# Third and fourth quarter's z: half of the reload moved from GpSimd's to ScalarE's queue and behind K's last spectra, three buffers instead of two, and a lower planned rate for those spectra

## The chip, the cores and the metric

The kernel runs on one core of one Trainium2 chip. The metric is the device time of one execution in microseconds (us). The kernel before has a median of 581.79 us in three runs (581.66 to 582.94).

## What is computed

Two independent blocks whose results are laid side by side. Block A is an FNet mixing layer, block B a long convolution (an S4D state-space layer), both for a sequence of 2048 and a width of 512, in float32:

```python
# A: y = Real(DFT_seq(DFT_hidden(x)))
a = einsum("bsd,ed->bse", x, dft_hid_re);  b = einsum("bsd,ed->bse", x, dft_hid_im)
y_A = einsum("ts,bse->bte", dft_seq_re, a) - einsum("ts,bse->bte", dft_seq_im, b)
# B: a convolution kernel K from the state-space parameters, applied by FFT
P = exp((A * dt[:, None])[:, :, None] * pos);  K = 2.0 * einsum("dn,dnl->dl", C, P).real
Kf = rfft(K, 2 * L);  Uf = rfft(u.transpose(0, 2, 1), 2 * L)
y_B = irfft(Uf * Kf, 2 * L)[:, :, :L].transpose(0, 2, 1) + u * D_skip
out = concatenate([y_A, y_B], axis=-1)
```

## The kernel before

**Block A** (`Fnet`) is dense matrix multiplication. Every float32 operand is split into a high and a low part: ScalarE writes `hi<-raw` (line 226), VectorE `lo<-raw,hi` (line 230), and three matmuls of 128x512 (line 371) make one product: `hi,x_hi`, `lo,x_hi`, `hi,x_lo`. Eight groups with the sequence matrix write intermediate tiles `p` to DRAM, and four last groups read them back as `raw<-p` (line 339, SyncE's queue), eight tiles to a group, and store `out_ya` (line 405). Four split tiles (`hi`, `lo`) exist at a time, so each `hi<-raw` waits until TensorE has used up the tile four before.

**Block B** (`Ssm`) builds K's taps with tables on VectorE and ScalarE, transforms u and K by an FFT in two stages, and works through the 512 channels in four quarters of 128 (`h` = 0 to 3). The parts near the change are these:

- `store_k` (line 879) writes the first stage of K's transform to DRAM, `xk<-xk_sb`. `load_spectrum` (line 990) reads u's and K's spectra back, four pieces (`q` = 0 to 3) to a quarter. For the last quarter the pieces go into 16 tiles that block A no longer needs, `x_hi8`, `x_lo8` to `x_hi15`, `x_lo15`, so K's last spectra are 16 transfers `x_hi<-xk` and `x_lo<-xk` of 128 KB, in rows of 128 floats (512 bytes), four to a piece, all on SyncE's queue.
- `product` makes the second stage with TensorE (line 1035, `f<-xt,w` or `f<-x_hi,w`), copies it with ScalarE (line 1014, `uk<-f`), multiplies the spectra on VectorE (lines 1019 to 1055), starts the inverse transform on TensorE (line 1062, `f<-uk,ia`), copies that with ScalarE (line 1077, `z<-f`), and `store_z` writes it to DRAM (line 1086, `zs<-z`, rows of 512 bytes). All these steps take turns in two pairs of PSUM banks, `f0` and `f1`: a step on TensorE waits until ScalarE has emptied the pair of the step before.
- `inverse2` (third and fourth quarter, `h` = 2 and 3) reads z back and finishes. A quarter has two passes, `i` = 0 and 1, and each pass loads 1 MB into a tile `zl` of 128 partitions: partitions 0 to 63 by one transfer of 512 KB on SyncE's queue, partitions 64 to 127 by another of 512 KB on GpSimd's queue (both line 1118), in rows of 1024 floats (4 KB). VectorE then adds and subtracts (lines 1124, 1126: `zsum<-zl`, `zl<-zl`), TensorE multiplies (line 1133, `f<-zsum,ib` and `f<-zl,ib`), ScalarE copies (line 1138, `zl<-f`), and the result is stored as `out_yb<-zl` (line 1141). The tiles `zl` and `zsum` have two buffers, so the fourth quarter's passes wait for the third quarter's stores.

**What sets the order.** A planner (`Plan`) runs all these steps as coroutines before the program is built. A step yields an engine and an estimated duration; the planner always takes the step that can start first, and the instructions are written out in that order. Each engine then runs its own instructions strictly in this order and waits by semaphores. A transfer is planned on one resource `"dma"` with a size and a rate: `load(512, 270)` stands for 512 KB at 270 KB per us. Planned numbers set only the order; no instruction waits for a planned time. A plan `Event` in the same way only holds a step back in the plan and leaves no semaphore behind.

All transfers on SyncE's and on ScalarE's queue share eight completion semaphores in turn, over both queues. A transfer therefore also waits until the one eight before it in the written order has landed. GpSimd's transfers have semaphores of their own.

Of the kernel before, what the change touches and what calls it, by code (L numbers as in the profile page):

```python
# [8 lines left out]
F32 = mybir.dt.float32  # L9
# [8 lines left out]
PART = DM // 4  # L18
# [57 lines left out]
class Sem:  # L76


    def __init__(self, n):
        self.free, self.waiting = [0.0] * n, []  # L80
# [107 lines left out]
def act(cols):  # L188
    return 0.09 + cols * 0.00085


def dve(cols, rate=1.0):
    return (66 + cols / rate) / 960


def load(kb, rate=330):
    return max(0.55, kb / rate)
# [211 lines left out]
class Buffers:  # L409


    def __init__(self, pool, n):
        self.pool, self.n = pool, n
        self.xts, self.uks, self.zbs, self.zls = Sem(1), Sem(n), Sem(n), Sem(n)


class Joined(Event):
# [18 lines left out]
class Ssm:  # L436
# [506 lines left out]
    def quarters(self):  # L943


        self.plan.spawn(self.constants(1, self.const2_ev), 3)
        self.zs_left, self.xt = [4] * 4, {}
        self.xt_ev = {(n, h, q): Event() for n in "uk" for h in range(4) for q in range(4)}
        self.take_ev = {(h, q): Event() for h in range(4) for q in range(4)}
        self.plan.spawn(self.take(), 1)  # L950
        xu = [self.xu[:, :, :, PART * h:PART * h + PART] for h in range(4)]
        self.plan.spawn(self.spectra("u", xu, [[self.xu_ev] * 2] * 4), 1)
        self.plan.spawn(self.spectra("k", [self.xk[h] for h in range(4)], self.xk_ev), 1)
        self.plan.spawn(self.products(), 1)
        self.ib2_ev = Event()
        self.plan.spawn(self.load_ib2(), 1)
        for h in range(4):
            self.plan.spawn(self.inverses(h), 1)
# [24 lines left out]
                self.plan.spawn(self.load_spectrum(name, h, q, view), 1)  # L983

    def load_spectrum(self, name, h, q, view):
        yield "dma", load(512, 270), FAST
        for r in range(2):
            for p, xt in enumerate(self.xt[h, q][r]):
                n = xt.shape[1]
                self.nc.sync.dma_start(xt[:, :, "uk".index(name)], view[2 * q + r, :, n * p:n * p + n])  # L990
        self.plan.set(self.xt_ev[name, h, q])

    def products(self):
        for h in range(4):
            yield self.set_ev[h // 3]
            b = self.sets[h // 3]
            for q in range(4):
                for n in "uk":
                    yield self.xt_ev[n, h, q]
                yield b.uks  # L1000
                got = yield from self.banks(2)
                done = Event()
                self.plan.spawn(self.product(b, h, q, got, done), LATE[h] if h < 3 else LAST)
                yield done
# [105 lines left out]
    def inverse2(self, b, h, i, n):  # L1110

        nc, c = self.nc, n // 2
        z = b.pool.tile([128, 2, c, PART], F32, name="zl", bufs=b.n)
        view = self.zs[h].rearrange("(a s) c l d -> (s c) a l d", a=2)
        yield "pool", ISSUE
        for y, e in enumerate((nc.sync, nc.gpsimd)):
            o = n * i + c * y
            e.dma_start(z[64 * y:64 * y + 64], view[:, :, o:o + c])
        yield "dma", load(64 * n, 270), FAST if h == 3 else None
        t = b.pool.tile([128, c, PART], F32, name="zsum", bufs=b.n)  # L1120
        for w in range(0, c, 4):
            m = slice(w, w + 4)
            yield "dve", dve(512)
            nc.vector.tensor_tensor(t[:, m], z[:, 0, m], z[:, 1, m], op=OP.add)
            yield "dve", dve(512), *APART
            nc.vector.tensor_tensor(z[:, 1, m], z[:, 0, m], z[:, 1, m], op=OP.subtract)
        (k, ps), = yield from self.banks(1)
        yield "pe", 1.06, None, 64
        for o in range(0, c, 2):
            for x in range(4):  # L1130
                for y in range(2):
                    r, w = slice(64 * y, 64 * y + 64), o + x // 2
                    nc.tensor.matmul(ps[32 * x:32 * x + 32, y, PART * (o // 2):PART * (o // 2) + PART],
                                     self.ib2[r, c * i + w, x % 2], (t, z[:, 1])[x % 2][r, w], start=True, stop=True,
                                     tile_position=(64 * y, 32 * x))
        for y in range(2):
            yield "act", act(512)
            nc.scalar.activation(z[:, 0, 4 * y:4 * y + 4].rearrange("p w d -> p (w d)"), ps[:, y], AF.Copy)
        self.give(k)
        yield "dma", load(32 * n, 270)  # L1140
        nc.sync.dma_start(self.out[:, c * i:c * i + c, PART * h:PART * h + PART], z[:, 0])
        self.plan.put(b.zls)
# [28 lines left out]
ISSUE = 1.0  # L1171
# [76 lines left out]
```

## Time and profile before

| what | value |
|---|---|
| median of three runs | 581.79 us |
| the profiled execution's own time | 582.32 us |
| its span in the profile | 580.5 us |
| TensorE (PE) busy | 570.5 us, 98% of the span |
| VectorE (DVE) busy | 523.0 us, 90% |
| ScalarE (ACT) busy | 371.2 us, 64% |
| GpSimd (POOL) busy | 42.5 us, 7% |
| moved by DMA | 133.70 MB, mean 230 GB/s |
| mean granted TensorE clock | 0.997 |

The profile is of one execution. Its span runs from the first to the last recorded instruction; the execution's own time, 582.32 us, is 1.8 us longer, and 0.53 us above the median of the three runs. Times in the rows are microseconds from the span's start. PE is TensorE's matmul side, PEld its weight loads, SPq and ACTq are the DMA issues on SyncE's and ScalarE's queue; DMA issues don't count as busy time. A row of the timeline gives the start, the duration, the engine, the line, the operation, the output and inputs, how many were merged, and in brackets how long the engine had been idle and what ended that.

### The profile page before, as it was taken

The numbers are of one execution on the slowest core, as the hardware profiler recorded it, in microseconds if no ns is written. First come the engines' busy times: TensorE is split into PE (matmuls) and PEld (weight loads), VectorE is DVE, ScalarE is ACT, GpSimd is POOL, SyncE is SP. The second block draws the span as 40 slices with busy tenths as digits, with TensorE's granted clock in tenths as the row PEclk, the third lists the DMA queues.
The fourth block names the chain that finished last, engine by engine and source line by source line (L and its number), as shares of the span: only waits on it lengthen the run. The fifth ranks groups of instructions, "written<-read, shape, count | busy, mean of one in ns | idle before, by whom it ended". The sixth has DMA issues, their size and how long they took to land.

```text
span 580.5 us, 15679 instructions
## 1 busy us (share of the span) xinstructions
PE 570.5 (98%) x6278; PEld 433.6 (75%) x6278; DVE 523.0 (90%) x928; ACT 371.2 (64%) x728; POOL 42.5 (7%) x64
## 2 busy tenths in 40 slices
PE   8999999999999999999999999999999999989997
PEld 6877767788777777778777777777787777756685
DVE  7999999999999999999999999999989999346742
ACT  5779665763777595768568585945688745335632
POOL 0001000000100000000000001001100000000000
PEclk9999999999999999999999999999999999989999
DMA  8899999996569767866796887479999995799784
GB/s 276 309 370 259 288 281 275 282 274 169 134 159 240 201 178 219 205 170 213 205 224 190 235 218 225 126 184 295 249 286 268 234 295 165 183 237 302 211 231 146
DMA packets 147976, 133.70 MB, mean 230 GB/s; under 512 B 47296, under 2 KB 107328, under 8 KB 147648
## 3 DMA queue, kind: packets, MB, share of 16 engines
q1 hardware_dynamic: 138976, 115.54, 66.8%
q0 software_dynamic: 8640, 16.78, 14.4%
q8 instruction: 49, 0.80, 0.6%
q10 hardware_dynamic: 288, 0.39, 0.2%
q14 instruction: 23, 0.19, 0.1%
HBM read 89.95 MB, written 42.73 MB: 229 GB/s over the span
## 4 chain that ended last, share of the span: by engine, by line
PE 59%; DVE 26%; DMA 6%; issue 5%; ACT 2%; SPq 1%; DVEq 0%; ACTq 0%
PE acc L371 46%; DVE prod L613 8%; DVE t L622 5%; PE f L1035 4%; DVE lo L230 4%; PE f L809 3%; PE f L1062 3%; DMA xk<-xk_sb 2%; DMA x_lo<-xk 2%; DVE t L642 1%; DMA raw<-in_sT 1%; DMA xu<-zl 1%; PE f L858 1%; PE f L1155 1%; DVE z L1019 1%
## 5 line engine op out<-in xcount | busy, mean ns | idle before, releaser
L371 PE MATMUL acc<-hi,x_hi 128*128 128x512 f32 x640 | 258.9, 404 | 0.1
L371 PE MATMUL acc<-lo,x_hi 128*128 128x512 f32 x640 | 250.7, 392 | 0.0
L371 PE MATMUL acc<-hi,x_lo 128*128 128x512 f32 x640 | 250.1, 391 | 0.0
L613 DVE TENSOR_TENSOR prod<-t,cs 128x1024 f32<-128x1024 f32 (+4 forms) x192 | 163.3, 869 | 1.7 <-ACT t L731 0.6
L371 PEld LDWEIGHTS acc<-hi,x_hi 128*128 128x128 f32 x640 | 120.6, 188 | 50.2 <-issue 24.2
L371 PEld LDWEIGHTS acc<-hi,x_lo 128*128 128x128 f32 x640 | 120.5, 188 | 26.2 <-DVE x_lo L230 0.3
L371 PEld LDWEIGHTS acc<-lo,x_hi 128*128 128x128 f32 x640 | 120.8, 189 | 23.1 <-DVE lo L230 0.2
L226 ACT ACTIVATE hi<-raw 128x512 fp32r<-128x512 f32 x132 | 82.6, 628 | 65.4 <-PE acc L371 48.0
L230 DVE TENSOR_TENSOR lo<-raw,hi 128x512 fp32r<-128x512 f32 x132 | 90.2, 685 | 23.9 <-ACT hi L226 23.7
L622 DVE TENSOR_TENSOR t<-prod 128x512 f32<-128x512 f32 (+4 forms) x192 | 94.3, 513 | 1.0
L629 ACT ACTIVATE square<-t 128x256 f32<-128x256 f32 (+1 forms) x64 | 36.7, 573 | 32.1 <-DVE t L622 29.3
L1014 ACT ACTIVATE uk<-f 128x1024 f32<-128x1024 f32 x32 | 31.2, 1018 | 17.7 <-PE f L1035 17.7
L325 POOL DMA_DIRECT2D lo<-in_sT x28 | 24.5, 874 | 213.3 <-ACT lo L323 44.2
L396 ACT ACTIVATE y<-acc 128x512 f32<-128x512 f32 x47 | 28.0, 595 | 11.0 <-PE acc L371 10.8
L809 PEld LDWEIGHTS f<-t,t 128*32 128x32 f32 x2048 | 29.5, 110 | 6.9 <-issue 4.7
L809 PE MATMUL f<-t,t 128*32 128x64 f32 x2048 | 32.4, 220 | 0.9 <-DVE t L622 0.4
L1019 DVE TENSOR_TENSOR z<-uk 128x512 f32<-128x512 f32 x32 | 21.9, 686 | 10.3 <-ACT uk L1014 9.5
L320 POOL DMA_DIRECT2D hi<-in_sT x28 | 15.8, 566 | 189.5 <-PE acc L371 113.2
L1077 ACT ACTIVATE z<-f 128x512 f32<-128x512 f32 x32 | 17.7, 590 | 12.6 <-PE f L1062 10.4
L642 DVE TENSOR_TENSOR t<-square 128x128 f32<-128x128 f32 (+1 forms) x64 | 24.8, 387 | 0.0
L1035 PE MATMUL f<-xt,w 64*32 64x256 f32 x768 | 23.5, 379 | 0.0
L1021 DVE TENSOR_TENSOR uk<-uk 128x512 f32<-128x512 f32 x32 | 22.1, 690 | 1.0
(102 smaller groups left out, 506.5 us busy)
## 6 DMA issues: line engine op xcount, KB each, us to landing
raw<-in_sT SPq DMA_DIRECT2D x99, 256.0 KB, 5.2
p<-y SPq DMA_DIRECT2D x32, 256.0 KB, 3.3
xk<-xk_sb SPq DMA_DIRECT2D x32, 256.0 KB, 5.3
zs<-z SPq DMA_DIRECT2D x32, 256.0 KB, 4.0
raw<-p SPq DMA_DIRECT2D x32, 256.0 KB, 4.2
hi<-in_sT POOLq DMA_DIRECT2D x28, 256.0 KB, 4.6
lo<-in_sT POOLq DMA_DIRECT2D x28, 256.0 KB, 5.0
xt<-xu SPq DMA_DIRECT2D x24, 256.0 KB, 4.9
```

The costliest lines, as they stand in the source:

```text
L226: self.nc.scalar.activation(hi, src, AF.Copy)
L230: self.nc.vector.tensor_tensor(lo, src, hi.bitcast(F32), op=OP.subtract)
L371: nc.tensor.matmul(acc[d], l[:, cols], r, start=k == 0 and n == 0, stop=k == len(items) - 1 and n == 2)
L396: self.nc.scalar.activation(y, ps, AF.Copy, scale=-1.0 if g[2] == 1 else 1.0)
L613: self.nc.vector.tensor_tensor(p.rearrange("p k d c m -> p k (d c) m"), src.rearrange("p d c l -> p (d c) l")[:, None, :, rows].to_broadca ...
L622: self.nc.vector.tensor_tensor(dst[:, :, :, rows], p[:, 0], p[:, 1, :, ::-1], op=OP.add)
L629: self.nc.scalar.activation(sq, t[:, :, :, m // 2:m], AF.Square)
L642: self.nc.vector.tensor_tensor(t[:, :, 0, m:2 * m:2], box[0][:, :, 0], box[0][:, :, 1], op=OP.subtract)
L809: nc.tensor.matmul(ps[32 * j:32 * j + 32, i], t1[:, d, c], t2[:, d, c], start=c == 0, stop=c == 1, tile_position=(0, 32 * j))
L1014: a.activation(uk[:, r].rearrange("p g c n d -> p g (c n d)"), p, AF.Copy)
L1019: v.tensor_tensor(P[0][:, r], t[:, r], u[:, r], op=OP.mult)
L1035: nc.tensor.matmul(got[r][1][32 * xx:32 * xx + 32, g, 256 * c:256 * c + 256], self.w2[rows, 2 * q + r, xx, 32 * c:32 * c + 32], xt[rows].r ...
```

## The change

Four edits, all in block B.

1. **The queue of z's second half.** In `inverse2` the transfer of partitions 64 to 127 is issued by ScalarE instead of GpSimd, planned as a step of 0.5 us on ScalarE ahead of the transfer's own planned time. The first half stays on SyncE's queue, but is written out after the planned transfer time is granted and not with the second half.
2. **The place of the third quarter's.** For `h` = 2 the plan holds these steps back until K's last spectra (`"k"`, quarter 3, piece 3) are planned, by the new event `loaded_ev`.
3. **Buffers.** `zl` and `zsum` of the last stage have three buffers instead of two (`2 * b.n - 1` with `b.n` = 2), and the plan's semaphore for them three places. In the earlier stage `b.n` is 1 and nothing changes.
4. **The planned rate.** K's spectra of the last quarter are planned at 200 KB per us instead of 270.

```diff
-        self.xts, self.uks, self.zbs, self.zls = Sem(1), Sem(n), Sem(n), Sem(n)
+        self.xts, self.uks, self.zbs, self.zls = Sem(1), Sem(n), Sem(n), Sem(2 * n - 1)
...
     def load_spectrum(self, name, h, q, view):
-        yield "dma", load(512, 270), FAST
+        yield "dma", load(512, 200 if h == 3 and name == "k" else 270), FAST
...
         self.plan.set(self.xt_ev[name, h, q])
+        if (name, h, q) == ("k", 3, 3):
+            self.plan.set(self.loaded_ev)
...
-        z = b.pool.tile([128, 2, c, PART], F32, name="zl", bufs=b.n)
+        z = b.pool.tile([128, 2, c, PART], F32, name="zl", bufs=2 * b.n - 1)
         view = self.zs[h].rearrange("(a s) c l d -> (s c) a l d", a=2)
-        yield "pool", ISSUE
-        for y, e in enumerate((nc.sync, nc.gpsimd)):
-            o = n * i + c * y
-            e.dma_start(z[64 * y:64 * y + 64], view[:, :, o:o + c])
+        if h == 2:
+            yield self.loaded_ev
+        yield "act", 0.5
+        nc.scalar.dma_start(z[64:], view[:, :, n * i + c:n * i + n])
         yield "dma", load(64 * n, 270), FAST if h == 3 else None
-        t = b.pool.tile([128, c, PART], F32, name="zsum", bufs=b.n)
+        nc.sync.dma_start(z[:64], view[:, :, n * i:n * i + c])
+        t = b.pool.tile([128, c, PART], F32, name="zsum", bufs=2 * b.n - 1)
```

The written order differs from before only from the first piece of the fourth quarter on. Three places show it. Numbers behind names tell tiles apart; they are not the same numbers in the two kernels. Lines from 992 on are two to three higher in the changed kernel.

**TensorE, where the fourth quarter begins** (`f<-x_hi8`, `f<-x_lo8` are the first piece of K's and u's last spectra, `acc` is block A). Before:

```order
L371 MATMUL acc_6782<-hi_6684,x_hi0_5234 128x512
L371 MATMUL acc_6782<-lo_6685,x_hi0_5234 128x512
L371 MATMUL acc_6782<-hi_6684,x_lo0_5235 128x512
L1035 MATMUL f1_6734<-x_hi8_6013,w2_113 32x256 x4
L1035 MATMUL f1_6734<-x_lo8_6014,w2_113 32x256 x4
```

After:

```order
L371 MATMUL acc_6778<-hi_6684,x_hi0_5234 128x512
L371 MATMUL acc_6778<-lo_6685,x_hi0_5234 128x512
L371 MATMUL acc_6778<-hi_6684,x_lo0_5235 128x512
L371 MATMUL acc_6761<-hi_6708,x_hi1_5443 128x512
L371 MATMUL acc_6761<-lo_6709,x_hi1_5443 128x512
L371 MATMUL acc_6761<-hi_6708,x_lo1_5444 128x512
L1037 MATMUL f1_6734<-x_hi8_6013,w2_113 32x256 x4
L1037 MATMUL f1_6734<-x_lo8_6014,w2_113 32x256 x4
```

Three more matmuls of block A (one product) stand ahead of the first piece, and the pieces behind it follow three later too. Further on, 15 matmuls of block A stand between the third and the fourth piece's `f<-uk,ia` where there were 12, and 12 between the third quarter's two passes where there were three.

**ScalarE, from the third piece's `uk<-f` to the last piece's `z<-f`.** Before:

```order
L226 ACTIVATE hi_7011<-raw_6701 128x512
L1077 ACTIVATE z_7030<-f1_6991 128x2x2x128
L1077 ACTIVATE z_7030<-f0_6999 128x2x2x128
L1014 ACTIVATE uk_7046<-f1_7039 128x1024
L1014 ACTIVATE uk_7046<-f0_7045 128x1024
L226 ACTIVATE hi_7093<-raw_6720 128x512
L1077 ACTIVATE z_7123<-f1_7088 128x2x2x128
L1077 ACTIVATE z_7123<-f0_7096 128x2x2x128
L226 ACTIVATE hi_7134<-raw_6769 128x512
```

After:

```order
L226 ACTIVATE hi_7005<-raw_6701 128x512
L1120 DMA zl_6950<-zs_107 64x2x1024
L1120 DMA zl_6951<-zs_107 64x2x1024
L1079 ACTIVATE z_7029<-f1_6994 128x2x2x128
L1079 ACTIVATE z_7029<-f0_6999 128x2x2x128
L226 ACTIVATE hi_7053<-raw_6720 128x512
L1016 ACTIVATE uk_7049<-f1_7042 128x1024
L1016 ACTIVATE uk_7049<-f0_7048 128x1024
L226 ACTIVATE hi_7135<-raw_6769 128x512
L1079 ACTIVATE z_7127<-f1_7092 128x2x2x128
L1079 ACTIVATE z_7127<-f0_7099 128x2x2x128
```

The third quarter's two transfers stand between a split and the second piece's `z<-f`, and two splits stand ahead of a copy that they stood behind. The fourth quarter's two (`zl_7230`, `zl_7262`) stand on ScalarE directly behind the third quarter's last copy `zl<-f`, with one split between them and three behind. GpSimd's four transfers of line 1118 are gone, and GpSimd has nothing left to do there.

**SyncE's queue, from the first piece's `zs<-z` to the third piece's.** Before:

```order
L1086 DMA zs_107<-z_6929 128x4x128
L339 DMA raw_6972<-p3_1_1_94 128x512
L1118 DMA zl_6910<-zs_107 64x2x1024
L1118 DMA zl_6911<-zs_107 64x2x1024
L339 DMA raw_7034<-p3_1_2_95 128x512
L1086 DMA zs_107<-z_7030 128x4x128
L1086 DMA zs_107<-z_7123 128x4x128
```

After:

```order
L1088 DMA zs_107<-z_6929 128x4x128
L339 DMA raw_6973<-p3_1_1_94 128x512
L1122 DMA zl_6950<-zs_107 64x2x1024
L1088 DMA zs_107<-z_7029 128x4x128
L339 DMA raw_7034<-p3_1_2_95 128x512
L339 DMA raw_7090<-p3_1_3_96 128x512
L1122 DMA zl_6951<-zs_107 64x2x1024
L1088 DMA zs_107<-z_7127 128x4x128
```

(Each `zs<-z` is two transfers that read alike; one is shown.) The second pass's first half (`zl_6951`) now stands behind the second piece's store and two block-A loads, and that store stands behind one z transfer instead of two.

More of the change, by code (lines that the diff above doesn't have):

```diff
@@ L954, in quarters @@
         self.plan.spawn(self.products(), 1)
-        self.ib2_ev = Event()
+        self.ib2_ev, self.loaded_ev = Event(), Event()
         self.plan.spawn(self.load_ib2(), 1)
```

## Prediction

> **What bounds the kernel now.** The page first: its first part names the busiest engine.
>
> ```profile
> PE 570.5 (98%) x6278; PEld 433.6 (75%) x6278; DVE 523.0 (90%) x928; ACT 371.2 (64%) x728; POOL 42.5 (7%) x64
> ```
>
> TensorE (PE) is busy for 570.5 of 580.5 us, so an edit that leaves the matmuls alone can win only where PE waits or runs slowly. The waits of PE, longest first, show where:
>
> ```profile
> PE f L1035 <- DMA x_hi<-xk: 1.7, 1, 1.7
> ...
> PE f L1035 <- DMA x_lo<-xk: 1.0, 1, 1.0
> ```
>
> Both are in one place, the first piece of the fourth quarter, where the second stage of K's transform waits for K's last spectra. The timeline of PE around it:
>
> ```profile
> 511.49 0.39 PE L371 MATMUL acc<-hi,x_lo 128*128 128x512 f32 x1
> 511.80 0.42 PE L1035 MATMUL f<-x_hi,w 64*32 64x256 f32 x4
> ...
> 514.59 0.64 PE L1035 MATMUL f<-x_hi,w 64*32 64x256 f32 x8 [1.69 <-DMA x_hi<-xk]
> 516.25 0.63 PE L1035 MATMUL f<-x_lo,w 64*32 64x256 f32 x4 [1.03 <-DMA x_lo<-xk]
> ...
> 521.13 0.42 PE L1035 MATMUL f<-x_hi,w 64*32 64x256 f32 x4
> ...
> 525.28 1.12 PE L1062 MATMUL f<-uk,ia 32*64 32x256 f32 x32
> ```
>
> The stretch from a piece's first `f<-x_hi` through the nine `acc` matmuls behind it appears twice. Undisturbed it lasts 525.28 - 521.13 = 4.15 us, with the waits 521.13 - 511.80 = 9.33 us. The disturbance costs 5.18 us, more than its 1.69 + 1.03 = 2.72 us of idle time. The table by stretches shows part of the rest (after PE's and PEld's busy time: DVE, ACT, POOL, then granted clock, DMA share, GB/s):
>
> ```profile
> 510.00:515.00 5.00, 3.31 (x49) 1.89 (x47) 2.29 (x4) 1.96 (x3) 0.00 (x0) 1.00 1.04 194
> 515.00:520.00 5.00, 3.97 (x35) 2.22 (x30) 1.17 (x3) 1.02 (x1) 0.00 (x0) 0.66 1.14 235
> ...
> 535.00:540.00 5.00, 5.00 (x79) 3.37 (x77) 2.00 (x4) 2.57 (x4) 0.00 (x0) 1.00 1.05 231
> 540.00:545.00 5.00, 5.00 (x74) 3.36 (x76) 4.96 (x9) 2.25 (x4) 0.00 (x0) 1.00 0.29 82
> ```
>
> Right behind the waits the granted clock averages 0.66 over 5 us, which is 0.34 x 5 = 1.70 us of work lost. The last 0.76 us are matmuls of the piece that normally overlap in pairs and were pulled apart.
>
> Why are the spectra late? The issues on SyncE's queue and GpSimd's, in order of time:
>
> ```profile
> 505.98 0.37 SPq L990 DMA_DIRECT2D x_hi<-xk  x1
> ...
> 506.91 0.46 SPq L990 DMA_DIRECT2D x_hi<-xk  x1
> 507.42 0.47 SPq L990 DMA_DIRECT2D x_lo<-xk  x1
> ```
> ```profile
> 507.43 1.26 POOL L1118 DMA_DIRECT2D zl<-zs  x2 [64.27 <-ACT y L396]
> ```
>
> These three take 3.8, 7.5 and 8.8 us from issue to landing, by the DMA view of a window around each issue:
>
> ```profile
> x_hi<-xk SPq DMA_DIRECT2D x1, 128.0 KB, 3.8
> ```
> ```profile
> x_hi<-xk SPq DMA_DIRECT2D x1, 128.0 KB, 7.5
> ```
> ```profile
> x_lo<-xk SPq DMA_DIRECT2D x1, 128.0 KB, 8.8
> ```
>
> What lies between them is GpSimd's issue of the third quarter's z halves, 1 MB in rows of 4 KB. By queue (packets, MB, share of the 16 engines' time), from 509 to 516 us:
>
> ```profile
> q0 software_dynamic: 265, 0.99, 73.1%
> q1 hardware_dynamic: 871, 0.42, 28.9%
> ```
>
> In these 7 us GpSimd's queue (q0) moves z's megabyte, and SyncE's queue (q1), which holds the spectra, gets 28.9% and 0.42 MB. That z is used only in the third quarter's passes, far behind (the chain further down); it comes early, and in the way.
>
> **The change part by part.** I count on the clock of before, as if the disturbance were there, and subtract it at the end.
>
> *Z leaves 507 us.* ScalarE's timeline of before shows the two steps between which z's halves now stand:
>
> ```profile
> 532.88 0.63 ACT L226 ACTIVATE hi<-raw 128x512 fp32r<-128x512 f32 x1 [1.10 <-PE acc L371]
> 534.02 1.09 ACT L1077 ACTIVATE z<-f 128x512 f32<-128x512 f32 x2 [0.50 <-PE f L1062]
> ```
>
> So they are issued behind a split that ran at 532.88, 25 us after GpSimd's issue. Nothing else but block A's loads shares the engines with K's spectra, so I take 3.8 us for the first piece's others too: the last, issued at 507.42, lands at 511.2. PE asks for it at 511.80 + 0.66 for the three matmuls put ahead = 512.5 at the earliest. The wait of 2.72 us goes, with the pulled-apart pairs and the low clock: -5.18 us. The lower planned rate matters only through those three matmuls, which are moved, not added: 0. From below: at 7.5 us it would land at 514.9; 2.4 us of waiting would stay, and 1.70 for the clock: 4.1.
>
> [...]
>
> *Two issues on ScalarE.* No row has this shape on ScalarE; on SyncE the same transfer takes 0.60 us to issue, at most 1.21.
>
> ```profile
> L1118 SPq DMA_DIRECT2D zl<-zs x4: 579/601/1205, 529.8 to 556.5; - x4
> ```
>
> Queued behind them is the second piece's `z<-f`, possible from 534.02 + 0.66 = 534.68. The split ends between 533.5 and 534.2 (it may move by 0.66 too); 1.2 us of issues make that 534.7 to 535.4, and the copy ends by 536.5. The fourth piece, which needs the banks, starts at 536.83 (next rows). Cost 0; at 1.21 us each up to 0.9 us; a gain is excluded, since PE has no gap here (5.00 of 5.00 from 535 to 540).
>
> *Z in its new place.* The chain from 536 us, in order of time:
>
> ```profile
> 536.17 1.89 PE f L1035 x64
> 538.05 2.29 PE acc L371 x9
> 540.35 1.05 PE f L1062 x32
> 541.40 2.95 PE acc L371 x12
> 544.35 1.05 PE f L1062 x32
> 545.39 1.59 PE acc L371 x6
> 546.99 1.09 PE f L1133 x64
> ```
>
> Three more matmuls are 2.95 - 2.29 = 0.66 us. In the new order the fourth piece starts at 536.83, its `f<-uk` at 536.83 + 1.89 + 2.29 + 1.05 + 2.95 + 0.66 = 545.67, the third quarter's first pass at 545.67 + 1.05 + 1.59 = 548.31, the second at 548.31 + 1.09 + 2.95 = 552.35.
>
> The tight one is the third piece's `z<-f`: it reuses a tile whose store, `zs<-z` of the second piece, must have landed, and it empties the banks for `f<-uk` at 545.67. It lasts 1.09 us, so the store may land at 544.58.
>
> ```profile
> 542.00 1.09 ACT L1077 ACTIVATE z<-f 128x512 f32<-128x512 f32 x2 [2.25 <-DMA zs<-z]
> ```
> ```profile
> 535.13 8.89 SPq L1086 DMA_DIRECT2D zs<-z  x4
> ```
> ```profile
> q1 hardware_dynamic: 318, 1.00, 101.3%
> ```
>
> Before, it was issued at 535.13 and landed at 542.00, behind 1 MB of z and one load. The third row is the queue's from 533 to 538 us: full, at 1.00 MB in 5 us. Now 1.5 MB of z compete with it, and the load (0.26 MB) stands behind: 542.00 + 0.66 + 0.52 / 0.2 - 0.26 / 0.2 = 543.96 (0.52 MB is one transfer). That is 0.6 us early: cost 0, and a store that landed sooner would win nothing, since PE has no gap there. Its cover is thin. From above I take the slowest spectrum under GpSimd's traffic, the last number here:
>
> ```profile
> DMA to landing us min/median/max: 3.2/7.0/10.3
> ```
>
> The pair's second store, issued some 0.5 us behind the first as the spectra are, would then land at 535.13 + 0.66 + 0.5 + 10.3 = 546.6, and PE would wait 546.6 + 1.09 - 545.67 = 2.0 us, plus 1.70 for the clock: 3.7.
>
> The second pass's first half now waits on SyncE's queue for a split after 536.83 (0.63 us, and about as long on VectorE) and is issued near 539. Z transfers take at most 10.4, and a step of VectorE's on z takes 0.68:
>
> ```profile
> DMA to landing us min/median/max: 7.2/8.3/10.4
> ```
> ```profile
> 565.88 0.68 DVE L1124 TENSOR_TENSOR zsum<-zl 128x512 f32<-128x512 f32 x1
> ```
>
> So it lands by 549.4, VectorE's four steps end at 549.4 + 2.7 = 552.1, and PE asks at 552.35. Cost 0; each us later would cost one.
>
> *The tail and the third buffer.* From here PE has the same work in the same order as before.
>
> ```profile
> 568.00 1.09 PE f L1133 x64
> ...
> 571.38 1.09 PE f L1133 x64
> ```
>
> Before, the last pass's z was there at 565.88 at the latest, VectorE needs 2.7 us, and PE asked at 571.38: 2.8 us of slack. ScalarE now issues behind the third quarter's last copy (552.35 + 1.09 + 1.09 = 554.5), the last by about 556.5. The third buffer lets the first go without the third quarter's store, and GpSimd's queue is left empty. Queued behind it are splits that PE first needs 42 matmuls after 553.44, at 0.22 us each near 562.7. Cost 0.
>
> The sum: the profiled execution's 582.32 - 5.18 = 577.14; the median lies 0.53 below that execution, so **576.6 us**.
>
> **The rivals.**
>
> *The congestion moves* (0.20). Z's megabyte shares the engines with stores in rows of 512 bytes, as it did with spectra; the DMA share from 535 to 540 is 1.05 already. The store lands past 544.58 and PE waits at 545.67. For it: a margin of 0.6 us. Against it: from 540 to 545 the share is 0.29, 3.5 us of room. Time from 577.2, where a wait of 0.6 us would show, to 576.6 + 3.7 = 580.3. [...]
>
> *The low clock stays* (0.04). If it came from no wait, 1.70 us remain: 578.3. [...] Against it: 0.66 stands in the stretch of the waits and 1.00 in those around it.
>
> *The spectra stay late* (0.06): the change would not do what it says. They wait for something else, and only the three matmuls help: 581.79 - 0.66 = 581.1. Against it: 3.8 us to landing against 7.5 us, with issues 0.93 us apart and GpSimd's traffic between them.
>
> *Slower: the fourth quarter's reload* (0.06). Two queues now carry its 2.1 MB beside two results `out_yb` of 0.52 MB and two `out_ya` of half that, 3.7 MB in all, after a stretch that is fuller than before. If they went at 0.2 MB per us from 552.35, z would be there at 570.9; VectorE's 2.7 us make 573.6, 5.6 late for PE's 568.00, plus 1.70 for the clock: 576.6 + 7.3 = 583.9. It decides from a landing after 568.00 - 2.7 = 565.3, and eats the whole gain from 565.3 + 5.18 - 1.70 = 568.8. Against it: the same bytes were there by 565.88.
>
> **How the numbers follow.** The forecast has 0.64; 576.6 is its time. The range goes from 576.0 (0.6 below, for the spread of runs and small waits) up to 580.7, the bound of the spectra at 7.5 us (576.6 + 4.1), which holds the first two rivals and leaves out 0.12. About 0.2%, 1.16 us, is what a measurement here can tell from no change: the line is 580.63. Faster: 0.64 + 0.20 + 0.04 = 0.88. Same: the late spectra, 0.06. Slower: 0.06.
>
> **What would show it.** Right: PE has no wait for `x_hi<-xk` or `x_lo<-xk`, the first spectra land in about 4 us, the clock is 1.00 throughout, and the DMA share at 540 to 545 fills up. Wrong: PE waits at the last piece's `f<-uk` with ScalarE's `z<-f` released by `zs<-z`; or PE waits at the third quarter's second pass, or the fourth's, for z.

## The result, and the profile after

| what | before | after |
|---|---|---|
| median | 582.11 us (7 runs, 581.66 to 583.41) | 578.68 us (7 runs, 577.52 to 580.89) |
| the profiled execution | 582.32 us, span 580.5 us | 578.43 us, span 576.6 us |

The ratio is 0.9935, with a 95% interval from 0.9916 to 0.9955: by the ratio the change wins 3.8 us (2.6 to 4.9), and the medians differ by 3.4. The forecast was 576.6 us from a gain of 5.18 us. So the sign and the place were right, and the gain was put 1.4 to 1.8 us too high. Most of the experiments ask which term of the sum that is.

The profile after, from its first part:

```profile
PE 567.8 (98%) x6278; PEld 432.5 (75%) x6278; DVE 523.1 (91%) x928; ACT 371.1 (64%) x728; POOL 40.2 (7%) x60
```

The two waits for K's last spectra, 1.7 and 1.0 us, are gone, and the list of PE's waits names none at all between 505 and 570 us. The DMA view of the changed kernel from 506 to 514 us says why (KB each, median us to landing):

```profile
x_hi<-xk SPq DMA_DIRECT2D x8, 128.0 KB, 3.4
x_lo<-xk SPq DMA_DIRECT2D x8, 128.0 KB, 3.5
```

The table by stretches (busy PE, PEld, DVE, ACT, POOL, then granted clock, DMA share, GB/s) answers to the rows of before:

```profile
510.00:515.00 5.00, 5.00 (x79) 3.56 (x77) 2.00 (x3) 2.26 (x4) 0.00 (x0) 1.00 0.92 268
515.00:520.00 5.00, 5.00 (x84) 3.37 (x77) 4.41 (x7) 3.39 (x5) 0.00 (x0) 1.00 1.01 308
...
540.00:545.00 5.00, 5.00 (x108) 3.44 (x106) 2.13 (x4) 3.75 (x7) 0.00 (x0) 1.00 0.86 220
```

Where 0.66 stood is 1.00, PE is full, and the gap in the DMA share at 540 (0.29 before) is filled. The chain of the changed kernel, in order of time, shows the first piece undisturbed, 517.48 - 513.30 = 4.18 us where 9.33 had been, and the steps that the prediction followed further down:

```profile
513.30 1.89 PE f L1037 x64
515.19 2.29 PE acc L371 x9
517.48 1.89 PE f L1037 x64
...
536.63 1.05 PE f L1064 x32
537.68 3.63 PE acc L371 x15
541.31 1.25 PE f L1064 x28
...
548.20 1.09 PE f L1136 x64
```

To compare executions I use one stretch, from the last first-stage matmuls of K (`f<-ks,f1k`, line 858) to the last copy of y on VectorE. Everything ahead of it is the same program in all kernels here. First the kernel before, then the changed one, PE's timeline and VectorE's:

```profile
494.88 1.12 PE L858 MATMUL f<-ks,f1k 32*64 32x256 f32 x32
...
576.82 0.42 DVE L389 COPY y<-acc 128x256 f32<-128x256 f32 x1 [8.20 <-PE acc L371]
```
```profile
495.63 1.12 PE L858 MATMUL f<-ks,f1k 32*64 32x256 f32 x32
...
572.65 0.42 DVE L389 COPY y<-acc 128x256 f32<-128x256 f32 x1 [6.79 <-DMA out_yb<-zl]
```

That is 81.94 us before and 77.02 after: 4.92 us of the 5.18 show in these two executions. But the changed kernel's execution had come 0.75 us later to the start of the stretch, and from the last y to the end of the span it takes 576.6 - 572.65 = 3.95 us, against 580.5 - 576.82 = 3.68.

### The profile page after: what moved, and what is told of

It reads as the page before. It is cut to its first block, busy times and chain, and to the rows that moved or that the text cites. A ratio compares the mean times of both kernels' runs of the same rounds, so it can differ in the third digit from the quotient of the medians.

```text
span 576.6 us, 15666 instructions
## 1 busy us (share of the span) xinstructions
PE 567.8 (98%) x6278; PEld 432.5 (75%) x6278; DVE 523.1 (91%) x928; ACT 371.1 (64%) x728; POOL 40.2 (7%) x60
## 4 chain that ended last, share of the span: by engine, by line
PE 53%; DVE 34%; issue 7%; DMA 3%; ACT 3%; SPq 0%; DVEq 0%; ACTq 0%
PE acc L371 41%; DVE prod L613 11%; DVE t L622 6%; DVE lo L230 5%; PE f L1037 4%; PE f L1064 3%; PE f L809 3%; DVE t L642 2%; DMA out_yb<-zl 1%; DVE cs L683 1%; DVE z L1021 1%; DVE uk L1023 1%; PE f L858 1%; DMA zl<-zs 1%; DVE zl L925 1%
```

## The experiments

Each stands beside runs of the kernel before on the same chip (medians 582.52, 582.97 and 582.89 us in three batches of 23, 17 and 23 executions). Ratios are to those.

**The changed kernel again.** The hold on the third quarter's z is switched off, since no quarter has the number 9:

```diff
-        if h == 2:
+        if h == 9:
             yield self.loaded_ev
```

> The changed kernel without the line that holds the third quarter's z behind K's last spectra. The planner puts every instruction of every engine where the changed kernel has it, so this is the changed kernel once more, under another name. Two theories of why the median gained 3.4 us and not the 5.2 of the sum. 'Spread': the missing part lies in the first 495 us, whose instructions are the same in all kernels here; then the stretch from the last first-stage matmuls of K (f L858) to the last copy of y lasts 76.7 to 77.3 us again (76.96 in the changed kernel, 81.87 before), and only what lies ahead of it differs; time 577.5 to 580. 'New stretch': the last 80 us of the new order vary; then that stretch comes out longer, 77.5 to 79 us, with PE waiting at the third or last piece's f<-uk for ScalarE's z<-f; time 578.5 to 581.

578.44 us (577.35 to 579.96), ratio 0.9926 [0.9897, 0.9955]. Its stretch:

```profile
494.80 1.12 PE L858 MATMUL f<-ks,f1k 32*64 32x256 f32 x32
...
571.54 0.42 DVE L389 COPY y<-acc 128x256 f32<-128x256 f32 x1 [6.17 <-DMA out_yb<-zl]
```

76.74 us, within 0.3 us of the changed kernel's. "New stretch" falls: the new order repeats well. Two things follow. The hold, one of the four edits, does nothing by itself here: the planner reaches these steps late in any case, because `inverses` waits for the table `ib2` (a later run moves that wait, and then z comes at 508 us). And most of what spreads between executions of the new order lies ahead of the stretch: over the fourteen profiles, whose instructions are the same up to there, its start lies between 494.40 and 497.25 us.

**The two halves of the change.** The changed kernel with the old rate, and the kernel before with the new rate alone:

```diff
-        yield "dma", load(512, 200 if h == 3 and name == "k" else 270), FAST
+        yield "dma", load(512, 270), FAST
```
```diff
-        yield "dma", load(512, 270), FAST
+        yield "dma", load(512, 200 if h == 3 and name == "k" else 270), FAST
```

> The changed kernel with K's last spectra planned at the old rate of 270, so that the three matmuls stay behind the first piece; z's halves are on ScalarE's queue and late, as in the changed kernel. 'Traffic' theory (z's megabyte under the spectra made the stall): no wait for x_hi<-xk over 0.5 us, granted clock 1.00, the stretch from f L858 to the last y 76.5 to 77.7 us, time within 0.7 us of the changed kernel's 578.7. Rival 'rate' (it is the later asking that cures the stall): the waits come back with 2 to 3 us and the time is 581 to 582.5.

> The kernel before with the lower planned rate alone: the three matmuls go ahead of the first piece, z stays on GpSimd's queue at 507 us. 'Traffic' theory: PE asks 0.66 us later and waits 2.72 - 0.66 = 2.1 us still, the granted clock behind it stays below 0.9, time 581.1 to 582.1, that is 0 to 1 us under the kernel before. Rival 'rate': the waits are gone and the time is 578 to 579.5.

Old rate: 578.87 us (577.61 to 580.88), ratio 0.9928 [0.9899, 0.9956], the changed kernel's. Rate alone: 582.86 us (580.97 to 584.19), ratio 1.0000 [0.9983, 1.0017], no gain, and just above the range of either theory; the interval (1 us either way) still holds the 0.66 us that the rival "the spectra stay late" gave the three matmuls. "Rate" falls: as far as these intervals let one see, the other edits, with z's place among them, are the whole of the gain. The rate alone leaves this wait of PE and this clock behind it:

```profile
515.25 0.42 PE L1035 MATMUL f<-x_lo,w 64*32 64x256 f32 x4 [1.63 <-DMA x_lo<-xk]
```
```profile
515.00:520.00 5.00, 4.75 (x89) 3.20 (x97) 3.25 (x6) 1.95 (x3) 0.00 (x0) 1.00 1.14 247
```

A wait of 1.63 us and a clock of 1.00: here the low clock, which "traffic" also expected, does not follow the wait.

**The kernel before, profiled twice more.**

> The kernel before, once more, for a second profile of it. Of its 40 executions timed so far 23 show a granted clock of 0.999 or 1.000 (median 581.9 us) and 15 one of 0.997 or less (median 584.5 us). Theory 'clock': the idle time for K's spectra is much the same in each (2.2 to 3.2 us), and the half clock behind it comes in some executions only: in one at 0.999 or more the stretch from f L858 to the last y lasts 81.94 - 1.70 = 80.2 us, give or take 0.5, in one at 0.997 or less 81.5 to 82.5. Rival 'stall': the idle time itself differs by 1 us and more between executions, and the clock follows it.

> The same kernel and the same two theories as in the run beside it: a third profile of the kernel before. Clock 0.999 or more: stretch 79.7 to 80.7 us, time 580.9 to 583; clock 0.997 or less: 81.5 to 82.5 us, time 582 to 585.

582.59 and 581.77 us, both at a clock of 1.00. The first piece from its first `f<-x_hi` to that of the second piece, with the waits for the spectra, then the stretch from 515 to 520 us, and the ends of the long stretch, in the first:

```profile
513.11 0.42 PE L1035 MATMUL f<-x_hi,w 64*32 64x256 f32 x4
...
515.18 0.64 PE L1035 MATMUL f<-x_hi,w 64*32 64x256 f32 x8 [0.98 <-DMA x_hi<-xk]
517.65 0.42 PE L1035 MATMUL f<-x_lo,w 64*32 64x256 f32 x4 [1.83 <-DMA x_lo<-xk]
...
520.91 0.42 PE L1035 MATMUL f<-x_hi,w 64*32 64x256 f32 x4
```
```profile
515.00:520.00 5.00, 2.99 (x38) 1.76 (x39) 1.55 (x3) 1.36 (x2) 0.00 (x0) 1.00 1.14 227
```
```profile
496.19 1.12 PE L858 MATMUL f<-ks,f1k 32*64 32x256 f32 x32
...
576.99 0.42 DVE L389 COPY y<-acc 128x256 f32<-128x256 f32 x1 [6.50 <-PE acc L371]
```

and the piece and the long stretch in the second:

```profile
512.50 0.42 PE L1035 MATMUL f<-x_hi,w 64*32 64x256 f32 x4
...
516.36 0.42 PE L1035 MATMUL f<-x_lo,w 64*32 64x256 f32 x4 [2.36 <-DMA x_lo<-xk]
...
519.65 0.42 PE L1035 MATMUL f<-x_hi,w 64*32 64x256 f32 x4
```
```profile
495.58 1.12 PE L858 MATMUL f<-ks,f1k 32*64 32x256 f32 x32
...
576.22 0.42 DVE L389 COPY y<-acc 128x256 f32<-128x256 f32 x1 [6.83 <-PE acc L371]
```

The waits are there, 0.98 + 1.83 = 2.81 and 2.36 us against 2.72, and the stretches are 80.80 and 80.64 us instead of 81.94. The first is 0.1 over what I expected, the second inside. "Clock" stands: the stall comes in each of the three profiles, the half clock in one.

The prediction's own measure can be taken in both: the piece lasts 520.91 - 513.11 = 7.80 and 519.65 - 512.50 = 7.15 us, where the sum had 9.33. Less the undisturbed 4.15 us, the disturbance costs 3.65 and 3.00 us instead of 5.18: the waits of 2.81 and 2.36, and a rest of 0.84 and 0.64 that I put down to the matmuls pulled apart (0.76 in the prediction; in an undisturbed piece of the kernel before an `f<-x_lo` starts 0.02 us behind its `f<-x_hi`, at 521.15 and 521.13 us), with nothing for the clock.

Over all 63 timed executions of the kernel before in the three batches, 36 have a granted clock of 0.999 or 1.000 and a median of 582.29 us, 25 one of 0.997 or less and 584.47 us; two lie between. Of 13 executions of the changed program none is below 0.998; their median is 578.56. (A mean clock doesn't say where the clock fell. In the changed kernel's profile, at 0.998, it is 1.00 in every 5 us up to 570 us and falls only at the end, where PE has little left to do.)

**Third z tile.** In the real program only, and then for the planner too:

```diff
-        z = b.pool.tile([128, 2, 4, PART], F32, name="z", bufs=b.n)
+        z = b.pool.tile([128, 2, 4, PART], F32, name="z", bufs=2 * b.n - 1)
```
```diff
-        self.xts, self.uks, self.zbs, self.zls = Sem(1), Sem(n), Sem(n), Sem(2 * n - 1)
+        self.xts, self.uks, self.zbs, self.zls = Sem(1), Sem(n), Sem(2 * n - 1), Sem(2 * n - 1)
```

(the other two places that take a tile named `z` alike; the second diff stands on top of the first).

> The changed kernel with a third tile for z in the last quarter; the planner still counts two, so every engine's order is that of the changed kernel, and only the real wait is looser: the third piece's z<-f waits for the first piece's store instead of the second's. In the kernel with the old rate that copy had been held 4.36 us by zs<-z and cost PE 0.4 us; in the changed kernel's profile it was held 1.06 us and cost nothing. Theory 'thin cover' (in other executions the store lands later and PE waits): the copy starts as soon as PE is done with f<-uk, the median comes out 0.5 to 1 us under the changed kernel's 578.7 (577.6 to 578.2) and the runs lie within 2 us. Rival 'spread elsewhere' (the missing microsecond lies ahead of 495 us): 578.2 to 579.2 and a spread of 3 us, as before.

> The third tile for z, and the planner knows of it: it puts the last f<-uk six block-A matmuls earlier, and the last passes earlier too, so z's reload is asked for up to 2.6 us sooner. With the same theories as the run with the third tile alone. 'Thin cover': 577.6 to 578.2, as there, since PE has no gap in either. Rival 'z late': PE waits 0.5 to 2 us at the fourth quarter's first pass, time 578.7 to 580.5.

578.48 us (577.85 to 579.77), ratio 0.9929 [0.9914, 0.9945], and 578.34 us (577.83 to 579.98), ratio 0.9932 [0.9916, 0.9947]: neither differs from the changed kernel. The third piece's copy on ScalarE in the changed kernel, in the one with the old rate, and in the one with the third tile alone:

```profile
540.31 1.08 ACT L1079 ACTIVATE z<-f 128x512 f32<-128x512 f32 x2 [1.06 <-DMA zs<-z]
```
```profile
538.49 1.08 ACT L1079 ACTIVATE z<-f 128x512 f32<-128x512 f32 x2 [4.36 <-DMA zs<-z]
```
```profile
539.65 1.06 ACT L1079 ACTIVATE z<-f 128x512 f32<-128x512 f32 x2
```

The hold by the store disappears as meant, and wins nothing that can be measured. "Thin cover" falls as the account of the missing time; "z late" falls as well, though in its profile VectorE uses the fourth quarter's reload as soon as it lands. No version here beats the changed kernel measurably.

**Two buffers for the reload.**

```diff
-        z = b.pool.tile([128, 2, c, PART], F32, name="zl", bufs=2 * b.n - 1)
+        z = b.pool.tile([128, 2, c, PART], F32, name="zl", bufs=b.n)
```

(and `zsum` and the planner's semaphore alike).

> The changed kernel with two buffers for z's reload instead of three. The prediction put the third buffer at nothing: 578.2 to 579.3, no wait of PE at the passes (f L1136). Rival: without it the fourth quarter's first half waits for the third quarter's out_yb to be stored, lands about 3 us later and PE waits 1 to 3 us for zl at the fourth quarter's first pass: 579.7 to 582.

579.25 us (578.43 to 579.61), ratio 0.9939 [0.9926, 0.9953], and no wait at `f` L1136. The interval overlaps with the changed kernel's. Whether the third buffer is worth nothing or up to half a microsecond stays open.

**Queue or time.** Four kernels issue the third quarter's second halves, 1 MB for its two passes, from one of the two queues at other times; the first halves stay on SyncE's queue, where all kernels here issue them between 524 and 542 us. On ScalarE's queue, ahead of the spectra's end (the wait for the table moved behind the issue), and behind the spectra (the same with the hold put back):

```diff
-            yield self.ib2_ev
+            yield self.set_ev[1]
...
-        if h == 2:
-            yield self.loaded_ev
-        yield "act", 0.5
+        yield "act", 0.5, FAST
         nc.scalar.dma_start(z[64:], view[:, :, n * i + c:n * i + n])
+        yield self.ib2_ev
```

> The changed kernel, but the third quarter's z halves are issued on ScalarE's queue early, among the copies of y near 508 us, which is within 1 us of where GpSimd issued them before; the new rate stays. 'Traffic' theory (which queue carries z is indifferent, only when it moves counts): PE waits 1.5 to 2.5 us for x_hi<-xk and x_lo<-xk, the granted clock falls below 0.9 behind it, the stretch from f L858 to the last y lasts 79.5 to 81.5 us, time 580.5 to 582. Rival 'queue' (GpSimd's queue in particular crowded SyncE's out): waits under 0.5 us, stretch 76.7 to 77.7, time 578 to 579.5.

> The changed kernel with z's halves on ScalarE's queue, but put behind the second piece's copies of uk, near 520.6 us, instead of 528.5: behind K's spectra, but under the stores of the first piece. It answers to the run with GpSimd's queue held behind the last spectrum (issue at 519.06, 585.4 us). Theory 'time': which queue carries the megabyte is indifferent, and at 520 it delays the first piece's zs<-z, which holds the second piece's z<-f: PE waits 1.5 to 3 us behind the second f<-uk, time 581 to 586. Rival 'GpSimd's queue': ScalarE's queue leaves the stores their share, no wait over 0.5 us, 578 to 579.5.

On GpSimd's queue, behind a small copy that reads a tile which must be there first, K's last spectrum or the second piece's `uk`:

```diff
         if h == 2:
             yield self.loaded_ev
+            x = self.xt[3, 3][1][1]
+            g = b.pool.tile([128, 1], F32, name="g", bufs=2)
+            nc.gpsimd.tensor_copy(g, x[:, 1, 1, :1])
-        yield "act", 0.5
-        nc.scalar.dma_start(z[64:], view[:, :, n * i + c:n * i + n])
+        yield "pool", ISSUE
+        nc.gpsimd.dma_start(z[64:], view[:, :, n * i + c:n * i + n])
```

(shown for the spectrum; for `uk` the plan holds z back until that copy, and the small copy reads its tile).

> The changed kernel, but z's halves go back to GpSimd's queue, and GpSimd first copies one column of K's last spectrum, so that it cannot issue them before that spectrum has landed (near 518 us). Theory 'time, not queue': no wait for x_hi<-xk or x_lo<-xk, granted clock 1.00 from 510 to 520, time 578 to 579.5, within 0.7 us of the changed kernel. Rival 'queue' (GpSimd's queue crowds out whatever lies beside it, here the first pieces' stores zs<-z and block A's loads): PE waits 1 us or more between 518 and 545 us, for a z<-f held by zs<-z or for a split held by raw<-p, time 580 to 582.5.

> GpSimd's queue again, in the order of the run held behind the last spectrum, instruction for instruction, but GpSimd's small copy now reads the second piece's uk, so that z is issued when ScalarE does it in the changed kernel (near 528.5 us). Theory 'time': no wait over 0.5 us in the fourth quarter, granted clock 1.00, 578 to 579.5. Rival 'GpSimd's queue': the second piece's store is held up as the first one's was at 519, the third piece's z<-f waits 4 us or more for zs<-z and PE 2 us or more, 581 to 586.

| z's second halves issued at | by | median | ratio to before |
|---|---|---|---|
| 507.43 us | GpSimd (before) | 582.11 us | |
| 508.14 us | ScalarE | 584.11 us | 1.0022 [0.9996, 1.0047] |
| 519.06 us | GpSimd | 585.40 us | 1.0031 [1.0008, 1.0054] |
| 519.12 us | ScalarE | 584.51 us | 1.0023 [1.0001, 1.0046] |
| 523.09 us | GpSimd | 584.18 us | 1.0009 [0.9982, 1.0036] |
| 528.54 us | ScalarE (after) | 578.68 us | 0.9935 [0.9916, 0.9955] |

The first median is of the seven runs beside the changed kernel; the ratios of the four others are to their own batches. The two runs put on record first, 508 us from ScalarE and 519 us from GpSimd, came out above both of their theories (at most 582 and 582.5 us). At 508 us "traffic" was right on the waits, 1.01 and 1.20 us for spectra, and wrong on the clock, which stayed at 1.00. At 519 us the wait that the rival "queue" named did come, but the run from ScalarE's queue at the same time has it too, 5.22 us where at most 3 were expected, so it doesn't speak for the queue. The run at 523 us missed its place: the second piece's `uk` is ready at 522 us, not at 528, so it says nothing on the queues at 528. The pair at 519 does compare the queues. GpSimd's issue, ScalarE's copy, PE's wait:

```profile
519.06 1.26 POOL L1123 DMA_DIRECT2D zl<-zs  x2 [0.34 <-issue]
```
```profile
534.44 1.08 ACT L1079 ACTIVATE z<-f 128x512 f32<-128x512 f32 x2 [4.99 <-DMA zs<-z]
```
```profile
535.09 0.42 PE L1037 MATMUL f<-x_hi,w 64*32 64x256 f32 x4 [2.30 <-ACT z L1079]
```

and the same three from ScalarE's queue:

```profile
519.12 1.64 ACTq L1120 DMA_DIRECT2D zl<-zs  x2
...
536.61 1.09 ACT L1079 ACTIVATE z<-f 128x512 f32<-128x512 f32 x2 [7.91 <-DMA zs<-z]
```
```profile
537.26 0.65 PE L1037 MATMUL f<-x_hi,w 64*32 64x256 f32 x4 [5.22 <-ACT z L1079]
```

(The first profile is of a mild execution: 581.62 us at a clock of 0.999, where nine of that kernel's twelve have 0.997 or less and the median is 585.40.) The first piece's store from issue to landing, with z at 519 us on GpSimd's queue and then in the changed kernel:

```profile
zs<-z SPq DMA_DIRECT2D x2, 256.0 KB, 9.5
```
```profile
zs<-z SPq DMA_DIRECT2D x2, 256.0 KB, 4.7
```

With z at 519 us on ScalarE's queue it is 10.7 us. From either queue, z's megabyte delays the first piece's store, that holds the second piece's `z<-f`, and PE waits for the banks. So no gain comes from the queue as such, for these two queues at 508 and at 519 us; at 528 us GpSimd's queue was not tried. Behind K's spectra is not enough: 519 and 523 us are as bad as 507, because another transfer that someone waits for takes the spectra's place. At 528.5 the one beside it is the second piece's store. It too is slow, 7.5 us from issue to landing. But before PE wants the banks of the copy that waits for it, it has 541.31 - 537.68 = 3.63 us of block A's work, 15 matmuls instead of nine. That this slack is what makes 528.5 a good place is read from the traces; no run varied the slack alone.

## Why the prediction was right, and where it was wrong

**What bounds it: right.** With z away, K's spectra land in 3.4 to 3.5 us (I had taken 3.8) and PE does not wait for them.

**The price of the disturbance: right for that execution, wrong for the median.** I subtracted 5.18 us from the profiled execution and set the median 0.53 us below it, as if each execution carried the whole sum. Measured over the stretch, that execution against the changed program's two gives 81.94 - (77.02 + 76.74) / 2 = 5.06 us. But the half clock, 1.70 us of the sum, is not in most executions: in the two profiles without it the disturbance costs 3.65 and 3.00 us. At a clock of 1.00 the stretch is 80.72 us (the mean of two), the gain 3.84 us, and with the tail that ends 0.3 us later about 3.5: 582.11 - 3.5 = 578.6 us, where 578.68 was measured. By clock, over all batches, the medians differ by 582.29 - 578.56 = 3.7 us in full-clock executions and 584.47 - 578.56 = 5.9 us in the others. **The failed step is the term of 1.70 us in the sum for the median.** The profile page of before had its sign: a mean clock of 0.997 is itself 0.003 x 580.5 = 1.7 us, and whether the median runs share it was not known. That the execution lay so near the median hid this: its stretch was 1.1 to 1.3 us longer than those of the two other profiles, but began 0.7 to 1.3 us earlier. Some tenths of a microsecond stay open: between the profiles with and without the half clock the disturbance differs by 1.5 and 2.2 us, but the whole stretch by only 1.1 and 1.3.

**The rival "low clock stays"** gave 578.3 us, the nearest number, but by luck: it said that the low clock stays, and the low clock does go away; it was mostly not there (36 of 63 executions have a granted clock of 0.999 or 1.000). The profiled execution of the kernel before by single microseconds:

```profile
516.00:517.00 1.00, 0.75 (x16) 0.43 (x20) 0.00 (x0) 0.00 (x0) 0.00 (x0) 0.67 1.15 188
517.00:518.00 1.00, 1.00 (x16) 0.21 (x4) 0.00 (x0) 0.00 (x0) 0.00 (x0) 0.50 1.18 231
518.00:519.00 1.00, 1.00 (x6) 0.81 (x3) 0.00 (x0) 0.79 (x1) 0.00 (x0) 0.50 1.20 292
519.00:520.00 1.00, 1.00 (x4) 0.77 (x4) 0.70 (x2) 0.24 (x1) 0.00 (x0) 0.63 1.15 278
```

The clock is at half for (0.33 + 0.50 + 0.50 + 0.37) / 0.5 = 3.4 us. It falls behind gaps of 1.69 and 1.03 us, with eight `f<-x_hi` between them; in the first of that kernel's two further profiles it stays at 1.00 behind gaps of 0.98 and 1.83 us. So the length of the gaps does not tell these two apart; what decides whether the clock falls is not shown.

**Two issues on ScalarE, cost 0: right.** They took 1.65 us, longer than the 1.2 I had allowed, and the next copy still waited for PE, not for them:

```profile
528.54 1.65 ACTq L1120 DMA_DIRECT2D zl<-zs  x2
530.36 1.09 ACT L1079 ACTIVATE z<-f 128x512 f32<-128x512 f32 x2 [1.25 <-PE f L1064]
```

**Z in its new place, cost 0: right, and as thin as said.** The store that I put 0.6 us ahead of its need held the copy 1.06 us; the copy then ended at about 541.4, PE asked at 541.31, and its `f<-uk` took 1.25 us instead of 1.05. With the old rate it did cost PE 0.4 us. "The congestion moves" (0.20) is therefore no invention: at 519 and 523 us it is the whole result. For the second pass I had PE ask at 552.35 on the clock of before, which is 552.35 - 5.18 + 0.75 = 547.9 here; it asked at 548.20 and did not wait.

**The rate and the three matmuls, cost 0:** not contradicted. Alone, the rate brings 0.0 us (-1.0 to +1.0); undone, it costs nothing measurable. **The third buffer, cost 0:** not contradicted. **The spectra stay late** (581.1) and **slower by the fourth quarter's reload** (583.9) did not happen: no wait for spectra, none at `f` L1136.

## What to carry to other kernels

A profile is one execution: before a term goes into a forecast of the median, ask whether every execution pays it, and a short fall of the granted clock is the first to ask of (here 3.4 us at half, in one profile of three). Here a large early reload that was in somebody's way was not cured by another queue, nor by just any later place, but by one where what flies beside it has slack (3.63 us at 528.5); list the transfers with a deadline around each candidate. And an engine whose queue runs ahead of the plan (GpSimd here, idle for 64.27 us ahead of its issue at 507.43) needs a real dependency, or an engine with other work in order, before a planned place means anything.

## What was not expected of the hardware

In the middle of the kernel two profiles show the half clock. It lasts 3.4 us in the kernel before, and about the wait of 5.22 us (z on ScalarE at 519) in these two stretches (0.45 + 0.23) x 5 / 0.5 = 6.8 us, twice as long:

```profile
535.00:540.00 5.00, 2.74 (x56) 1.50 (x64) 0.69 (x1) 2.28 (x4) 0.00 (x0) 0.55 0.44 118
540.00:545.00 5.00, 5.00 (x66) 2.89 (x50) 4.26 (x7) 1.38 (x2) 0.00 (x0) 0.77 0.90 236
```

There PE stopped at 537.26 - 5.22 = 532.04 us; by single microseconds the clock falls at about 535.5 (0.75 from 535 to 536, then 0.50), 3.5 us later, and is back at about 542.3 (0.83 from 542 to 543). In the kernel before it fell at about 516.3, with no such stop ahead of it.

With z on ScalarE at 508 us, SyncE's queue stopped issuing spectra for 515.85 - 510.64 = 5.2 us, and the list of its waits names z (total, times, longest):

```profile
508.14 2.90 ACTq L1118 DMA_DIRECT2D zl<-zs  x2
```
```profile
510.17 0.47 SPq L990 DMA_DIRECT2D x_hi<-xk  x1
515.85 0.36 SPq L990 DMA_DIRECT2D x_lo<-xk  x1
```
```profile
SPq L990 <- DMA zl<-zs: 5.7, 2, 5.2
```

In the traces of the kernel before and of the changed one, none of the 432 and 436 transfers of these two queues that follow another on one of the eight semaphores is issued before that one has landed. A slow z ahead in this turn fits the wait that the list names: the first one landed 7.7 us after its issue, at 508.14 + 7.7 = 515.8 us. In the kernel before the list names no z there, and SyncE's issues wait at most 2.2 us, for spectra; GpSimd's early z instead took the larger share of the engines. By queue, 512 to 516 us, first before, then with z on ScalarE (q10):

```profile
q0 software_dynamic: 170, 0.61, 79.4%
q1 hardware_dynamic: 373, 0.18, 28.1%
```
```profile
q1 hardware_dynamic: 1050, 0.51, 79.2%
q10 hardware_dynamic: 98, 0.34, 33.7%
```

Two ways to be late, and about the same time in the end.
